# Reordered products, copies on either of two engines, and more buffers at the end of a fused attention and feed-forward kernel

## The chip, the core and the metric

The kernel runs on one core of a Trainium2 chip. A core has TensorE (PE in the profile, with its weight loads as PEld), VectorE (DVE), ScalarE (ACT), GpSimd (POOL) and SyncE (SP, which here only issues transfers). PE writes its sums to PSUM, of which this kernel uses eight banks; ACT and DVE read them from there. The engines run side by side, each through its own queue in a fixed order, and wait for one another by semaphores. The metric is the time of one execution in microseconds (us) as the device measures it; smaller is better. The span in a profile is some 1.8 us shorter than that time.

## The reference

```python
# q, k, v: 8 x 12 x 448 x 64; x: 3584 tokens x 768; d_ff = 2048
attn = softmax(rmsnorm(q) @ rmsnorm(k).T / 8) @ v
x = attn.transpose(0, 2, 1, 3).reshape(B * S, H * D)
h = x @ w_in
g = h * (1 / (1 + exp(-1.702 * h)))
return g @ w_out
```

The change touches only the last line and what surrounds it.

## The kernel before

For each batch of 448 tokens the kernel projects x (16 blocks of 6 matmuls), gets the gate as h * (1 + tanh(0.851 h)) with ACT and DVE, and multiplies by w_out with matmuls of 384 columns. The factor 0.5 comes with the copy out of PSUM. Attention for later batches runs between these matmuls.

`g @ w_out` is done for two tiles of 128 tokens at a time, as 2x2 blocks with seven products in place of eight. Four of the seven (P1, P6, P7, P4) add into one bank, and each intermediate value of that bank is itself needed. So it has to be copied out (X1, X2, X3) before the next product may add to it:

```python
def copy(name, tm, hf, after, **kw):                 # always on ACT
    od.add(name, "ACT", 490, lambda: copy_out(a, bp, tm, hf), ..., deps=[(*after, 1)], **kw)
def p6():
    multiply(P(6), a, S2, T2, False, None, [S2, X(1)] + terms)
    copy(X(2), t1, 1, P(6), takes=("osb", [...]))
def p7():
    multiply(P(7), a, S3, T3, False, None, [S3, X(2)])
    copy(X(3), t2, 1, P(7), takes=("osb", [...]))
    ...
def p4():
    multiply(P(4), a, A(3), T4, False, None, [X(3)])
    ...
def s():                                             # sums of gates, on DVE; 3 buffers
    summing(S1, A(2), A(3), ALU.add, b, (*P(5), 1))
    summing(S2, S1, A(0), ALU.subtract, b, (*P(6), 1))
    summing(S3, A(2), A(0), ALU.subtract, b, (*P(7), 1))
    summing(S4, A(1), S2, ALU.subtract, b, (*P(3), 1))
```

The products' order is written by hand for each kind of batch. A and B are the pairs, C is the one tile that has no partner, in four products; `s` stands for the sums:

```python
EVEN = ["s", 1, 2, 5, 6, 7, 4, 3]
FIRST = order("As A1 A2 A5 A6 Bs B1 A7 A4 A3 B2 B5 B6 B7 B4 B3")
MIDDLE = order("As A1 A2 A5 A6 C0 A7 C1 A4 A3 C2 Bs B1 B2 B5 B6 C3 B7 B4 B3")
FINAL = order("As A1 C0 A2 A5 A6 C1 A7 C2 Bs A4 A3 C3 B1 B2 B6 B5 B7 B8 B4")
```

Every operation goes as a task, with an estimated duration, to a planner in the kernel's own Python code. It plays the engines through, gives each free engine the ready task with the smallest key, and emits the instructions in the order in which it started them. The queues on the chip then run in that order, whatever the real times are. The planner keeps tasks marked `lock` (the sums are) away from POOL's work in its own timeline; nothing on the chip does.

## Time and profile before

| | before |
|---|---|
| time, median of the first 3 runs (range) | 433.37 us (432.29 to 433.52) |
| span of the profiled run | 431.6 us |
| PE busy | 412.6 us (96%), 3874 matmuls |
| DVE, ACT, POOL busy | 275.6, 317.2, 189.5 us |
| clock granted to PE (1.00 is full speed), first 17 us / from there to the last matmul | 0.90 / 1.00 |

The prediction below shows the lines that carry the argument. Beside them, the rows of the two instruction groups that empty PSUM. A row gives line, engine, operation, written<-read, shapes, count, then busy us, mean ns of one, and the engine's idle time before them with what ended most of it.

```profile
L961 ACT ACTIVATE osb<-w 128x384 f32<-128x384 f32 x45 | 22.1, 490 | 24.4 <-PE w L951 21.7
...
L965 DVE SCALAR_TENSOR_TENSOR osb<-w,osb 128x384 f32<-128x384 f32 x27 | 15.0, 554 | 20.4 <-PE w L951 11.0
```

Both engines mostly wait for PE here, as they should when PE sets the time.

### The profile page before, as it was taken

How to read it: one execution, taken by the hardware profiler on the slowest of the kernel's cores; microseconds unless marked ns; L12 is line 12 of the kernel's file. 1: busy time of each engine (PE TensorE's matmuls, PEld its weight loads, DVE VectorE, ACT ScalarE, POOL GpSimd, SP SyncE). 2: the span in 40 equal slices, each digit the busy share in tenths (PEclk: the TensorE clock that was granted, in tenths of full speed). 3: DMA queues.
4: the chain of work that ended last, by engine and by line, in shares of the span. 5: the costliest groups of instructions: out<-in, count | busy, mean ns of one | idle time of the engine just before them, and what ended most of it. 6: DMA issues, size and time to landing. Idle time of an engine off the chain costs nothing.

```text
span 431.6 us, 10059 instructions
## 1 busy us (share of the span) xinstructions
PE 412.6 (96%) x3874; PEld 242.7 (56%) x3874; DVE 275.6 (64%) x549; ACT 317.2 (73%) x472; POOL 189.5 (44%) x277
## 2 busy tenths in 40 slices
PE   6999899999999999999999899999999999999995
PEld 4558686655555555555555455555555555554553
DVE  4967988589977568857685447756564345635522
ACT  4798798869988889888877778878866676524221
POOL 5486943657648585463447353554624001000000
PEclk9899999999999999999999999999999999999999
DMA  9999999574795996785468895464326431030032
GB/s 208 240 257 245 257 247 248 139 163 99 162 211 149 208 229 144 182 190 153 97 158 192 167 202 120 118 173 119 83 73 152 99 90 21 12 85 0 18 93 73
DMA packets 101555, 63.38 MB, mean 147 GB/s; under 512 B 54916, under 2 KB 101508, under 8 KB 101508
## 3 DMA queue, kind: packets, MB, share of 16 engines
q1 hardware_dynamic: 93712, 55.88, 54.6%
q0 software_dynamic: 7296, 6.29, 8.9%
q8 instruction: 30, 0.49, 0.5%
q10 hardware_dynamic: 500, 0.57, 0.4%
q14 instruction: 17, 0.14, 0.1%
HBM read 45.61 MB, written 11.01 MB: 131 GB/s over the span
## 4 chain that ended last, share of the span: by engine, by line
PE 81%; ACT 6%; DVE 5%; DMA 4%; issue 2%; POOL 0%; SPq 0%; DVEq 0%; ACTq 0%; POOLq 0%
PE w L864 30%; PE w L951 20%; PE o L653 11%; PE sc L632 9%; PE w L894 4%; PE sc L951 3%; PE sc L864 3%; DMA raw<-in_k_dram 2%; ACT att L642 2%; ACT sq L514 1%; PE w L588 1%; ACT osb L961 1%; DVE g L886 1%; ACT att L640 1%; DVE late L942 1%
## 5 line engine op out<-in xcount | busy, mean ns | idle before, releaser
L640 ACT ACTIVATE att<-sc 112x896 bf16<-112x896 f32 x168 | 146.8, 924 | 23.5 <-PE sc L632 23.2
L864 PE MATMUL w<-xt,w_in_s 128*128 128x448 bf16 (+1 forms) x804 | 149.1, 330 | 0.5 <-DVE g L886 0.4
L864 PEld LDWEIGHTS <-w_in_s 128*128 128x128 bf16 x864 | 78.0, 97 | 53.3 <-issue 6.2
L565 POOL TENSOR_TENSOR row<-raw,rs 112x512 bf16<-112x512 f32 x80 | 86.5, 1103 | 29.6 <-DMA qk<-row 17.6
L653 PEld LDWEIGHTS <-att 112*128 112x128 bf16 x1536 | 72.0, 98 | 44.8 <-issue 19.0
L886 DVE SCALAR_TENSOR_TENSOR g<-th,w 128x448 bf16<-128x448 f32 x118 | 71.9, 616 | 28.9 <-ACT th L874 28.6
L874 ACT ACTIVATE th<-w 128x448 f32<-128x448 f32 x118 | 65.7, 558 | 23.6 <-PE w L864 20.5
L578 POOL TENSOR_TENSOR vx<-vraw,ones 112x512 bf16<-112x512 f32 x35 | 38.7, 1104 | 89.3 <-PE o L653 59.4
L653 PE MATMUL o<-vx,att 112*128 112x65 bf16 x1280 | 73.4, 194 | 1.1 <-DVE obs L664 1.0
L523 DVE TENSOR_REDUCE ssq<-sq 112x16 f32<-112x1024 f32 (+1 forms) x50 | 58.6, 1173 | 14.8 <-ACT sq L514 14.1
L514 ACT ACTIVATE sq<-raw 112x1024 f32<-112x1024 f32 (+1 forms) x43 | 44.8, 1041 | 10.1 <-DMA raw<-in_k_dram 6.2
L951 PEld LDWEIGHTS <-late 128*128 128x128 bf16 x376 | 33.7, 97 | 26.0 <-issue 7.6
L632 PE MATMUL sc<-qk 64*128 64x448 bf16 (+1 forms) x360 | 47.5, 344 | 0.9 <-DVE qk L595 0.5
L663 DVE RECIPROCAL rcp<-o 112x4 f32<-112x4 f32 x96 | 17.1, 178 | 43.6 <-PE o L653 43.4
L664 DVE TENSOR_TENSOR obs<-o,rcp 112x256 bf16<-112x256 f32 x96 | 40.7, 424 | 3.3
L951 PEld LDWEIGHTS <-g 128*128 128x128 bf16 x336 | 30.1, 97 | 22.2 <-issue 5.5
L961 ACT ACTIVATE osb<-w 128x384 f32<-128x384 f32 x45 | 22.1, 490 | 24.4 <-PE w L951 21.7
L951 PE MATMUL w<-w_out_s,g 128*128 128x384 bf16 x192 | 36.1, 326 | 0.0
L951 PE MATMUL w<-w_out_s,late 128*128 128x384 bf16 x168 | 32.8, 326 | 1.2 <-DVE osb L965 1.2
L951 PE MATMUL w<-late 128*128 128x384 bf16 x160 | 31.1, 326 | 1.2 <-ACT osb L961 1.2
L965 DVE SCALAR_TENSOR_TENSOR osb<-w,osb 128x384 f32<-128x384 f32 x27 | 15.0, 554 | 20.4 <-PE w L951 11.0
L555 POOL TENSOR_TENSOR t<-rs 112x48 f32<-112x48 f32 x28 | 8.2, 292 | 40.5 <-DVE rs L544 39.4
(77 smaller groups left out, 367.0 us busy)
## 6 DMA issues: line engine op xcount, KB each, us to landing
raw<-in_q_dram SPq DMA_DIRECT2D x44, 224.0 KB, 4.2
raw<-in_k_dram SPq DMA_DIRECT2D x43, 224.0 KB, 4.6
vraw<-in_v_dram SPq DMA_DIRECT2D x42, 224.0 KB, 3.8
w_in_s<-in_moe_w_in_dram POOLq DMA_DIRECT2D x4, 768.0 KB, 15.8
w_out_s<-in_moe_w_out_dram POOLq DMA_DIRECT2D x4, 768.0 KB, 21.6
out_dram<-osb SPq DMA_DIRECT2D x14, 168.0 KB, 2.5
out_dram<-osb SPq DMA_DIRECT2D x16, 144.0 KB, 2.3
out_dram<-osb SPq DMA_DIRECT2D x16, 120.0 KB, 2.7
```

The costliest lines, as they stand in the source:

```text
L514: nc.scalar.activation(out=sq[i % N_SQ][:SS, part], in_=raw[turn(i, N_RAW, K_RAW)][:SS, part], func=ACT.Square)
L523: nc.vector.reduce_sum(out=ssq_of[g0][:SS, i - g0, part], in_=sq[i % N_SQ][:SS, part], axis=AX.X)
L565: eng.tensor_tensor(out=row_ring[i % N_QKN][:SS, gi].rearrange("p n (h d) -> p h n d", h=2), in0=raw[turn(i, N_RAW, K_RAW)][:SS, gi], in1= ...
L578: nc.gpsimd.tensor_tensor(out=vx[:, :, :D], in0=vr, in1=ones[:SS, :].to_broadcast([SS, 2 * NS, D]), op=ALU.mult)
L632: nc.tensor.matmul(sc[:, hp, j * SH:j * SH + n], lhsT=qkw[r, k0:k0 + WIN], rhs=qk[r, 0, qs], start=True, stop=True)
L640: nc.scalar.activation(out=att[:SS, t, :, :S], in_=sc, func=ACT.Exp)
L653: nc.tensor.matmul(os_[u, w][:, x, :], lhsT=att_of(u)[:SS, kc, hp, qs * SS:qs * SS + WIN], rhs=vx_ring[turn(i, N_V, K_V)][:SS, hp, kc, :], ...
L664: nc.vector.tensor_tensor(out=to[:SS, :, w, :] if h is None else to[:SS, :2].rearrange("p n h d -> p (n h) d"), in0=o[:SS, :, :D], in1=rcp ...
L864: nc.tensor.matmul(gps[b, m][:, j * SH:j * SH + n], lhsT=w_in_s[:, ki, f * 128:(f + 1) * 128], rhs=xT[b][:, ki, lo:lo + n], start=(ki == 0 ...
L874: nc.scalar.activation(out=th[:, :], in_=gps[b, m][:, :S], func=ACT.Tanh, scale=0.851)
L886: nc.vector.scalar_tensor_tensor(out=g_of[b // 2][:, f:f + len(g), lo:lo + n], in0=view(ths.pop((b, m))[:, :]), scalar=1.0, in1=view(gps.p ...
L951: nc.tensor.matmul(held[to], lhsT=lhs[:, ko, :], rhs=y[:, ko, :], start=first and ko == 0, stop=ko == NK - 1, skip_group_check=not first)
```

## The change

The intent is that no product follows directly on the copy of its bank's partial sum. For that, half of C moves to the even batches, the next batch's first projection (D) is cut in two and pulled in, and the last batch interleaves A and B. A copy may run on ACT or DVE, whichever the planner finds free. Products wait for their own precomputed weight term only, and the subtractions that make those terms (`TT`) lose precedence. After attention, its idle buffers serve as more store buffers (osb) and sum buffers. The core of the diff:

```diff
-    EVEN = ["s", 1, 2, 5, 6, 7, 4, 3]
-    FIRST = order("As A1 A2 A5 A6 Bs B1 A7 A4 A3 B2 B5 B6 B7 B4 B3")
-    MIDDLE = order("As A1 A2 A5 A6 C0 A7 C1 A4 A3 C2 Bs B1 B2 B5 B6 C3 B7 B4 B3")
-    FINAL = order("As A1 C0 A2 A5 A6 C1 A7 C2 Bs A4 A3 C3 B1 B2 B6 B5 B7 B8 B4")
+    FIRST = order("As A1 A2 A5 A6 Bs B1 A7 A4 A3 B2 B5 B6 D0 B7 D1 B4 B3")
+    EVEN = order("As A1 A2 A5 A6 C0 A7 C1 A4 A3")
+    MIDDLE = order("As A1 A2 A5 A6 C2 A7 C3 A4 A3 Bs B1 B2 B5 B6 D0 B7 D1 B4 B3")
+    FINAL = order("As A1 B1 A2 A5 A6 C2 A7 Bs C3 A4 A3 B2 B6 B5 B7 B8 B4")
 ...
-                   deps=[(*after, 1)], **kw)
+                   deps=[(*after, 1)], either=("DVE", 560, lambda: copy_out_v(a, bp, tm, hf)), **kw)
 ...
-            multiply(P(7), a, S3, T3, False, None, [S3, X(2)])
+            multiply(P(7), a, S3, T3, False, None, [S3, X(2)] + term(0))
 ...                                                  # likewise P5, P6, P4
-                           10.3 + done / PACE - 2, lock=True,          # the terms TT
+                           10.3 + done / PACE + TERM_LATE, lock=True,  # TERM_LATE = 1.0
 ...
+            od.add("later", "none", 0, lambda: None, 0,
+                   widen=[("osb", len(osb_ring)), ("sums", len(sums))],
+                   deps=last_values(NG - 1))
```

(`...` marks cuts; the copies of `C` get the same choice of engine.) The rest of the diff teaches the planner to offer one task to two engines and to pick the buffer that has been free longest.

More of the change, by code (lines that the diff above doesn't have):

```diff
@@ L20 @@
 class _Task:
-    __slots__ = ("eng", "dur", "lat", "emit", "key", "after", "at", "takes", "left", "users", "end", "start", "lock", "widen", "moves", "rest", "there", "alt")
+    __slots__ = ("eng", "dur", "lat", "emit", "key", "after", "at", "takes", "left", "users", "end", "start", "lock", "widen", "moves", "rest", "there", "alt", "either")
 OVERLAP = {"ACT": 95.0, "DVE": 90.0, "POOL": 45.0}
@@ L41, in add @@
     def add(self, name, eng, dur, emit, key, deps=(), lat=100.0, at=0.0, takes=None,
-            lock=False, widen=None, moves=None, alt=None):
+            lock=False, widen=None, moves=None, alt=None, either=None):
         t = _Task()
@@ L57, in add @@
         t.moves = moves
+        t.either = either and (either[0], either[1] - OVERLAP[either[0]],
+                               lat - OVERLAP.get(eng, 0.0) + OVERLAP[either[0]], either[2])
         t.key = KEYS.get(name, round(key, 3))
@@ L127, in run @@
                         c = heapq.heappop(q)
+                        if c[2].end is not None:
+                            continue
                         if self._fits(c[2], now):
@@ L135, in run @@
                         break
+                    if best.either and eng != best.eng:
+                        best.eng, best.dur, best.lat, best.emit = best.either
+                    best.either = None
                     if best.takes and best.takes[0] in self.loose:
@@ L142, in run @@
                         self.slots[best.takes[0]][1].extend(best.takes[1])
-                    if best.widen:
-                        self.slots[best.widen[0]][0] = best.widen[1]
+                    for name, n in best.widen or ():
+                        self.slots[name][0] = n
                         self.fill = None
@@ L177, in run @@
                 for u in t.users:
-                    if (u.eng == t.eng) == same:
+                    if (u.eng == t.eng and not u.either) == same:
                         u.left -= 1
@@ L184, in run @@
                 seq += 1
-                heapq.heappush(ready[t.eng], (t.key, seq, t))
+                for eng in (t.eng, t.either[0]) if t.either else (t.eng,):
+                    heapq.heappush(ready[eng], (t.key, seq, t))
         move_to(now + 1e6)
@@ L460 @@
     th_p = pool("th", 3)
-    osb_p = pool("osb", 6)
+    osb_ring = ring("osb", 6, [128, HALF], FP32)
+    for t in att_ring:
+        flat = t[:, :, :, :].rearrange("p n h q -> p (n h q)").bitcast(FP32)
+        osb_ring += [flat[:, j * HALF:(j + 1) * HALF] for j in range(NS)]
     ps_sc = pool("ps_sc", 1, space=PSUM)
@@ L468 @@
         od.slot(name, n)
-    od.loose = ("w",)
+    od.loose = ("w", "osb", "sums")
     banks = [ps_w.tile([128, 512], FP32, tag=f"w{j}", name=f"w{j}") for j in range(3)]
@@ L923 @@
     sums = [piece(S_LEN).rearrange("p (k t) -> p k t", k=NK) for _ in range(N_SUM)]
+    for t in sq:
+        flat = t[:, :, :, :, :].rearrange("p g h n d -> p (g h n d)").bitcast(BF16)
+        sums += [flat[:, j * S_LEN:(j + 1) * S_LEN].rearrange("p (k t) -> p k t", k=NK)
+                 for j in range(2)]
     B11, T1, B21, B22 = [w_out_s[:, NK * r:NK * r + NK, hf * HALF:(hf + 1) * HALF]
@@ L932 @@
     od.slot("sums", N_SUM)
-    sum_of, summed = {}, [0]
+    sum_of = {}
     def tokens(bp, tm, r):
@@ L938, in add_up @@
     def add_up(name, x, y, op):
-        sum_of[name] = sums[summed[0] % N_SUM]
-        summed[0] += 1
+        sum_of[name] = sums[od.got]
         x, y = (sum_of[t] if t in sum_of else tokens(*t) for t in (x, y))
@@ L956, in half_of @@
         if (bp, tm, hf) not in osbs:
-            osbs[bp, tm, hf] = osb_p.tile([128, HALF], FP32, tag="osb", name="osb")
+            osbs[bp, tm, hf] = osb_ring[od.got]
         return osbs[bp, tm, hf][:, :]
@@ L961, in copy_out, with copy_out_v @@
         nc.scalar.mul(half_of(bp, tm, hf), held[frm], 0.5)
+    def copy_out_v(frm, bp, tm, hf):
+        nc.vector.tensor_scalar(out=half_of(bp, tm, hf), in0=held[frm], scalar1=0.5, scalar2=None,
+                                op0=ALU.mult)
     def add_out(frm, bp, tm, hf):
@@ L973 @@
     PACE = 5800.0
+    TERM_LATE = 1.0
     END = (B // 2 - 1, 2 * S // 128 - 1)
-    EVEN = ["s", 1, 2, 5, 6, 7, 4, 3]
     order = lambda text: [(p[0], int(p[1]) if p[1:].isdigit() else p[1]) for p in text.split()]
-    FIRST = order("As A1 A2 A5 A6 Bs B1 A7 A4 A3 B2 B5 B6 B7 B4 B3")
-    MIDDLE = order("As A1 A2 A5 A6 C0 A7 C1 A4 A3 C2 Bs B1 B2 B5 B6 C3 B7 B4 B3")
-    FINAL = order("As A1 C0 A2 A5 A6 C1 A7 C2 Bs A4 A3 C3 B1 B2 B6 B5 B7 B8 B4")
+    FIRST = order("As A1 A2 A5 A6 Bs B1 A7 A4 A3 B2 B5 B6 D0 B7 D1 B4 B3")
+    EVEN = order("As A1 A2 A5 A6 C0 A7 C1 A4 A3")
+    MIDDLE = order("As A1 A2 A5 A6 C2 A7 C3 A4 A3 Bs B1 B2 B5 B6 D0 B7 D1 B4 B3")
+    FINAL = order("As A1 B1 A2 A5 A6 C2 A7 Bs C3 A4 A3 B2 B6 B5 B7 B8 B4")
     done = 0.0
@@ L982 @@
     last_sum = None
+    rest = []
     def plain(bp, b, tm, hf):
@@ L1032, in pair @@
         A = lambda j: (bp, (t1, t2)[j // 2], j % 2)
-        terms = [("TT", j, r) for j in range(4) for r in range(2)]
+        term = lambda j: [("TT", j, r) for r in range(2)]
         U = lambda tm, hf: ("U", bp, tm, hf)
@@ L1054, in p5 @@
         def p5():
-            multiply(P(5), c, S1, T1, True, U(t1, 1), [S1] + terms)
+            multiply(P(5), c, S1, T1, True, U(t1, 1), [S1] + term(1))
         def p6():
-            multiply(P(6), a, S2, T2, False, None, [S2, X(1)] + terms)
+            multiply(P(6), a, S2, T2, False, None, [S2, X(1)] + term(2))
             copy(X(2), t1, 1, P(6), takes=("osb", [("D", bp, t1, 1)]))
         def p7():
-            multiply(P(7), a, S3, T3, False, None, [S3, X(2)])
+            multiply(P(7), a, S3, T3, False, None, [S3, X(2)] + term(0))
             copy(X(3), t2, 1, P(7), takes=("osb", [("D", bp, t2, 1)]))
@@ L1067, in p4 @@
         def p4():
-            multiply(P(4), a, A(3), T4, False, None, [X(3)])
+            multiply(P(4), a, A(3), T4, False, None, [X(3)] + term(3))
             copy(U(t2, 0), t2, 0, P(4), takes=("osb", [("D", bp, t2, 0)]))
@@ L1106, in part @@
                        10.3 + done / PACE - 2, deps=[(*y[j], 1)],
+                       either=("DVE", 560, lambda: copy_out_v(to[hf], bp, tm, hf)),
                        takes=("osb", [("D", bp, tm, hf)]))
@@ L1110, in single, with project @@
         return [lambda j=j: part(j) for j in range(4)]
+    def project(b, m, kis):
+        nonlocal done, last
+        name = ("F", b, m) if kis[-1] == KI - 1 else ("F", b, m, kis[0])
+        od.add(name, "PE", len(kis) * 191, lambda: first(b, m, kis), 10.3 + done / PACE,
+               deps=[("X", b * NP + p, None if b else m // 8) for p in kis]
+               + [("WI", blocks(b, m)[0][0] // 4), last],
+               lat=250, takes=("w", [("G", b, m)]) if kis[0] == 0 else None,
+               widen=[("w", 3)] if b == m == 0 else None)
+        last = name
+        done += len(kis) * 191
     for b in range(B):
@@ L1115 @@
             key = 10.3 + done / PACE
-            od.add(("F", b, m), "PE", KI * 191, lambda b=b, m=m: first(b, m, range(KI)), key,
-                   deps=[("X", b * NP + p, None if b else m // 8) for p in range(KI)]
-                   + [("WI", blocks(b, m)[0][0] // 4), last],
-                   lat=250, takes=("w", [("G", b, m)]),
-                   widen=("w", 3) if b == m == 0 else None)
-            last = ("F", b, m)
-            done += KI * 191
+            if ("F", b, m) not in od.named:
+                project(b, m, range(KI))
             od.add(("H", b, m), "ACT", 542, lambda b=b, m=m: tanh(b, m), key - 2,
@@ L1131 @@
         if b == B - 1:
-            od.add("late", "none", 0, lambda: None, 0, widen=("w", len(banks)),
+            od.add("late", "none", 0, lambda: None, 0, widen=[("w", len(banks))],
                    deps=[("E", NG - 1, None, t) for t in range(NS)])
+            od.add("later", "none", 0, lambda: None, 0,
+                   widen=[("osb", len(osb_ring)), ("sums", len(sums))],
+                   deps=last_values(NG - 1))
         if b == 0:
@@ L1148 @@
                 one, two = pair(bp, b, 3, 4), pair(bp, b, 5, 6)
-                rest = single(bp, b, 2) if bp else []
+                next_first = [lambda kis=range(j, j + KI // 2): project(b + 1, 0, kis)
+                              for j in (0, KI // 2)]
                 for part in (FINAL if b == B - 1 else MIDDLE) if bp else FIRST:
-                    {"A": one, "B": two, "C": rest}[part[0]][part[1]]()
+                    {"A": one, "B": two, "C": rest, "D": next_first}[part[0]][part[1]]()
                 before_g = [last, last_sum]
@@ L1154 @@
                 one = pair(bp, b, 0, 1)
-                for j in EVEN:
-                    one[j]()
+                rest = single(bp, b, 2) if b > 0 else []
+                for part in EVEN:
+                    {"A": one, "C": rest}[part[0]][part[1]]()
     global _last_order
```

## The prediction

> **What bounds the kernel now.** I read the busy shares, the chain that ended last, what TensorE (PE) waits for after 94 us, and then the order of time around each wait. The first two say that PE sets the time:
>
> ```profile
> PE 412.6 (96%) x3874; PEld 242.7 (56%) x3874; DVE 275.6 (64%) x549; ACT 317.2 (73%) x472; POOL 189.5 (44%) x277
> ...
> PE 81%; ACT 6%; DVE 5%; DMA 4%; issue 2%; POOL 0%; SPq 0%; DVEq 0%; ACTq 0%; POOLq 0%
> ```
>
> The span is 431.6 us, so PE is idle for 19.0 us. By stretches of the span, 7.0 us of that lie before 70 us (the filling of the pipeline), 4.3 us after 425 us (the last copy and stores), and about 7.7 us in between, where the products that the change orders run (line L951, from 122 us on). PE's clock is full from 20 us on. No matmul goes away, so the change can win only what PE loses in between. Who holds PE up from 94 us on (total us, times, longest):
>
> ```profile
> PE w L951 <- ACT osb L961: 3.3, 5, 1.5
> PE w L951 <- DVE osb L965: 1.2, 2, 0.6
> PE o L653 <- DVE obs L664: 1.0, 1, 1.0
> PE sc L951 <- DVE osb L965: 0.7, 1, 0.7
> PE sc L951 <- ACT osb L961: 0.6, 1, 0.6
> PE w L864 <- DVE g L886: 0.4, 1, 0.4
> ```
>
> Nine waits, 5.8 us, are for a copy (L961) or an addition (L965) out of PSUM. This undercounts: a matmul of 384 columns is drawn 0.326 us long, but the next starts 0.162 us after it. From start to start, beyond that pitch, the nine cost 0.74 (at 144 us), 0.75 (236), 1.68 (245), 0.48 (283), 0.74 (336), 0.48 (379), 0.74 (381), 0.74 (419) and 0.87 us (421): 7.24 us in all. This is the ceiling for the reordering. One of them in order of time, products A6, A7 and A4 of batch 6, all on one bank:
>
> ```profile
> 378.73 1.46 PE L951 MATMUL w<-late 128*128 128x384 bf16 x8 [0.32 <-ACT osb L961]
> ...
> 380.22 0.49 ACT L961 ACTIVATE osb<-w 128x384 f32<-128x384 f32 x1 [1.55 <-PE w L951]
> ...
> 380.76 1.46 PE L951 MATMUL w<-late,g 128*128 128x384 bf16 x8 [0.58 <-ACT osb L961]
> ```
>
> A7 ends its last pitch near 380.02, the copy starts 0.2 us later, takes 0.49, and A4, which adds into the same bank, starts 0.05 us after that: 0.74 us lost each time a product follows its own partial sum's copy. The longest wait has another cause:
>
> ```profile
> 243.85 1.06 ACT L514 ACTIVATE sq<-raw 112x1024 f32<-112x1024 f32 x1 [1.34 <-DMA raw<-in_k_dram]
> ...
> 244.81 0.47 ACT L961 ACTIVATE osb<-w 128x384 f32<-128x384 f32 x1
> ...
> 245.34 1.46 PE L951 MATMUL w<-late,g 128*128 128x384 bf16 x8 [1.52 <-ACT osb L961]
> ```
>
> Here the copy sat in ACT's queue behind a square that waited for a load. At 236 and 336 us PE waits for an addition that frees one of the three banks: the single tile's sum (C2, C3) holds a bank across B1, B2 and B5. At the end two waits follow each other in the chain:
>
> ```profile
> 418.60 0.50 ACT osb L961
> 419.10 1.60 issue
> 420.69 0.57 DVE osb L965
> 421.26 0.04 issue
> 421.30 3.42 PE sc L951 x20
> ```
>
> B1 ended at 417.75, but its copy started at 418.60, 0.2 us after the fourth matmul of B2, and B2's fifth waited for that copy. B1 and B2 lay in the two halves of one two-bank sc tile, and the waits look set for the whole tile.
>
> **What the Trainium skill says.** "Perfetto Trace Analysis", section Matmuls, says that independent groups should rotate through different PSUM banks, so that one's evacuation overlaps the next one's matmuls. The trace agrees: only products that need the bank or the sum being read stop (0.74 us). "ScalarE: Activation LUTs", section What ACT_TABLE_LOAD costs, gives an ACTIVATE with immediate scale and bias 186 ns + 0.833 ns per element: 506 ns for 384, where the trace has 490. For a copy on DVE there is no row of before; the addition L965 reads the same bank and takes 554 ns, so I take 0.56 us. "PSUM — Partial Sum Buffer", section on bank collisions, wants guards by bank, not by address; the waits at 419 us are coarser still, by tile of two banks.
>
> **The change part by part.** It adds and removes no matmul (projecting a batch's first block in two halves of 3 matmuls keeps all 6), so PE's work stays as it is.
>
> 1. Even batches 2, 4 and 6 run "A6 C0 A7 C1 A4" for "A6 A7 A4". A product of 8 x 0.162 = 1.30 us covers the 0.2 + 0.49 + 0.05 = 0.74 us of a copy. The waits at 283, 379 and 381 us go: -1.7 us.
> 2. The odd batches before the last get the single tile's rest between A's products, so no third bank is held across B. The waits at 236 and 336 us go: -1.5 us.
> 3. "B6 D0 B7 D1 B4" puts 3 projection matmuls, 3 x 0.189 = 0.57 us, after a copy that needs 0.74 to 0.81. At 144 us some 0.2 us stay, -0.5. At 245 us the cause was a queue; the cover and the free choice of engine should take half to all of 1.68: -0.9. The projection's input lands in time: the last transposes before these points landed near 139 and 237 us, D1 comes near 146 and 244.
> 4. The last batch: B1 comes early, so its copy is long done when B2 and B6 run, -0.74. B6 still follows B2 at once, and the addition out of B2's bank can stop it again if both lie in one sc tile; I count half of 0.87, -0.4.
> 5. The terms' subtractions on DVE (8 of 1.0 to 1.2 us) lose their precedence over the gates of batch 1. PE waited for gates at 104 (0.29 us) and 110 us (0.73 us), beside these subtractions. -0.7. Each product now waits only for its own term, which permits this.
> 6. Copies on DVE: up to all 50, 50 x 0.56 = 28 us on an engine busy for 276 of 432. It fits. In the last copy of all it could cost 0.07 us.
> 7. More store and sum buffers, only once attention is over. ACT waited 6.4 us for stores near the end, but PE then had other banks: 0. The sums let S4 of B come sooner; PE never waited for it: 0.
>
> A cost: in batches 3 and 5 the order is now "A5 A6 C2", with still three sum buffers. C2's sum S5 comes after S4 in DVE's order; S4 gets the buffer that A5 frees, so S5 gets the one that A6 frees. C2 follows A6 directly, so it starts 0.2 + 0.69 (one L942 addition) + 0.05 = 0.94 us late, unless attention's matmuls fill the hole. Two such places, half filled: +1.0 us. For new accidents in the queues, like the one at 245 us, I add 0.5 us.
>
> Sum: 1.7 + 1.5 + 1.4 + 1.1 + 0.7 = 6.4 saved, 1.5 lost; net 4.9, from 433.4 to 428.5 us. Half of the accidents and refills may go well, so I put the middle at 428.2.
>
> **The rivals.** (a) Everything goes: the nine waits, the two for gates and the one for obs (1.16 us from start to start, at 281 us) are 9.4 us: 424.0 us. For it: PE's queue is otherwise full, attention offers work until 380 us. Against it: the order is fixed ahead from estimated times, and a static order always meets a late load somewhere. (b) The wait moves: C2 waits for S5, DVE's copies queue behind reductions that wait for ACT's squares (1.22 us each), projections hold banks longer, sc tiles collide more often. Then 3 to 4 us come back: 430 to 432 us. For it: DVE is 78% busy from 94 to 150 us, and the S5 dependence is plain in the code. (c) Attention becomes the bound, since products move forward from odd to even batches and projections are pulled up. ACT is 92% busy from 94 to 150 us. If projections then wait for transposes, 434 us or more. Against it: the input lands about 7 us before the pulled-up projections, and even batches get 2.6 us more time before the next projection.
>
> **Range and chances.** PE's removable loss bounds the win at 9.4 us, 2.2%; going 2% faster, below 424.7 us, needs nearly all of it, hence 0.04. Slower by 2%, above 442, needs a new stall bigger than any in this trace: 0.02. Repeats of before lie within 1.2 us, so the range comes from how many waits return: 425.5 to 431.5 us, the lower end with about 8 us won, the upper with about 2.
>
> **What would show it.** PE's waits for L961 and L965 should fall from 5.8 us to under 2, with none in even batches and none near 236 or 336 us. PE's busy time should stay within 1 us of 412.6, with the same 3874 matmuls. The new DVE copies should take 0.54 to 0.57 us, and L961's count fall by their number. A wait of C2 on L942 in batches 3 and 5, near 220 and 320 us, would show the cost I added. The tail after the last matmul should stay about 4.4 us. I am wrong if PE waits for transposes or gates more than before, if sc-tile waits in the last 30 us grow, or if the early part before 94 us shifts: the change should leave it as it is.

## The result

The changed kernel took 428.34 us (median of 4 runs, 428.1 to 428.48), the kernel before, on the same chip, 432.91 us. The ratio is 0.9894, with a 95% interval of 0.9876 to 0.9912. Such a ratio is the mean time of one kernel's runs over that of the other's of the same rounds, so it is not quite the ratio of the medians. It is faster by about 1%, clear of noise, and the forecast was 428.2 us.

The added code shifts the line numbers. In the kernel before, L951 is a product of `g @ w_out`, L961 a copy, L965 an addition out of PSUM, L942 a sum of gates, L653 attention's product with v, and L664 the division that follows it. In the changed kernel these are L965, L975 (copy on ACT) and L978 (copy on DVE), L983, L956, L664 and L675. L864 and L875 are the projection.

From the page of the changed kernel (span, busy times, shares of the chain that ended last):

```profile
span 426.3 us, 10048 instructions
...
PE 409.1 (96%) x3874; PEld 241.7 (57%) x3874; DVE 297.3 (70%) x584; ACT 302.6 (71%) x437; POOL 189.8 (45%) x277
...
PE 78%; DVE 11%; ACT 5%; issue 3%; DMA 2%; POOL 0%; DVEq 0%
```

PE still sets the time, with the same 3874 matmuls. The 35 copies that moved show as 35 more instructions on DVE (549 to 584) and 35 fewer on ACT (472 to 437). DVE's share of the chain rose from 5 to 11%. What PE waited for from 94 us on points to the reason (us in total, times, longest; it is the whole answer).

```profile
PE o L664 <- DVE obs L675: 4.7, 7, 1.2
PE w L965 <- DVE late L956: 0.2, 1, 0.2
```

All nine waits for copies and additions are gone. Seven waits for attention's division (obs) have come in place of one. In the chain after 94 us, sums of gates rose from 3.6 to 15.8 us. The end, where the chain before had copies, additions and "issue" between the products, is now one unbroken row of products. The chain of the changed kernel from 400 us on (start, us, what):

```profile
401.18 1.30 PE w L965 x8
402.48 2.60 PE sc L965 x16
...
418.08 3.91 PE sc L965 x24
421.99 0.02 issue
422.02 0.56 DVE att L978
```

**A measure that leaves out the start.** The first 1082 matmuls are the same in both kernels, yet the two profiled runs were already 1.27 us apart at the hundredth. The windows show the granted clock in the first 17 us as 0.90 in the run of before and 1.00 in the other. So 1.27 of the 5.2 us between the two spans is chance. From the thousandth matmul's start to the last one's, I get 339.98 us before and 335.91 after: the change itself is worth 4.07 us. This measure repeats well: the changed kernel gave 335.91 and 335.94 in two profiles on two occasions, and the kernel of e7 and e11 gave 331.19 both times. It holds where PE's clock stays full.

**Where those 4.07 us come from.** Each figure is the time from one matmul's start to the next beyond the usual pitch of that pair, summed by what ended the wait:

| PE lost, us (times) | before | after |
|---|---|---|
| copies and additions (L961, L965 / L975, L978, L983) | 7.23 (9) | 0 |
| attention's division (obs) | 1.16 (1) | 5.87 (7) |
| sums (L942 / L956) | 0 | 0.32 (1) |
| gates | 1.36 (4) | 0.24 (1) |
| other waits | 0.76 (4) | 0 |
| sum | 10.51 | 6.43 |

The difference is 4.08 us, which is all of it as far as this method can tell: waits of 0.1 us lie at its edge, so the row of others could be a few tenths larger or smaller. The change did what it was made for, and over half of the gain went into a new wait.

**The new wait, one place.** Timeline of the changed kernel in batch 2 (start, us, engine, line, operation, shapes, count, idle before and releaser):

```profile
176.25 3.94 POOL L576 TENSOR_TENSOR row<-raw,rs 112x512 bf16<-112x512 f32 x3
...
176.81 1.02 DVE L956 TENSOR_TENSOR late<-g 128x1024 bf16<-128x1024 bf16 x1
...
177.87 1.42 DVE L956 TENSOR_TENSOR late<-late,g 128x1024 bf16<-128x1024 bf16 x1
...
179.21 1.53 DVE L956 TENSOR_TENSOR late<-g 128x1024 bf16<-128x1024 bf16 x1
...
180.66 0.54 DVE L983 SCALAR_TENSOR_TENSOR osb<-w,osb 128x384 f32<-128x384 f32 x1
...
181.33 0.42 DVE L675 TENSOR_TENSOR obs<-o,rcp 112x256 bf16<-112x256 f32 x1
...
181.81 0.43 PE L664 MATMUL o<-vx,att 112*128 112x65 bf16 x8 [0.82 <-DVE obs L675]
```

The same three sums in the kernel before:

```profile
177.06 0.69 DVE L942 TENSOR_TENSOR late<-g 128x1024 bf16<-128x1024 bf16 x1
177.78 0.69 DVE L942 TENSOR_TENSOR late<-late,g 128x1024 bf16<-128x1024 bf16 x1
178.39 0.68 DVE L942 TENSOR_TENSOR late<-g 128x1024 bf16<-128x1024 bf16 x1
```

The planner takes 690 ns for a sum. That holds while POOL is idle, as it was before until 178.65 us. Beside POOL's work the three took 1.02, 1.42 and 1.53 us. They stand ahead of the division in DVE's queue, with an addition of 0.54 us between, and attention has one PSUM bank, which the division frees. Six of the seven waits, 5.5 of 5.87 us, have two or three sums ahead of the division, at least one of them slow; in four of the six an addition stands there too. Before the seventh (0.34 us, at 323 us) DVE was idle. "SBUF — State Buffer", section Who interferes with whom, says that a DVE instruction with two SBUF inputs contends with a GpSimd instruction that reads SBUF, and that the loser is blocked outright. The traces agree that they contend (whether the loser is blocked or only slowed, durations alone do not tell): of the 53 sums in both profiles that no POOL instruction overlaps, none took more than 0.694 us. Of the 41 that one overlaps, 29 took 0.74 to 1.55 us. Eleven sums before and 16 after took over 0.8 us. POOL's instructions are slowed too: L576 takes 1.04 us by the median and up to 1.5 us beside sums in the changed kernel. No run took POOL's work away, so that POOL is the cause rests on this overlap and on the page.

### The profile page after: what moved, and what is told of

The parts are those of the page before. It is cut to its first block, busy times and chain, and to the rows that moved or that the text cites. A ratio compares the mean times of both kernels' runs of the same rounds, so it can differ in the third digit from the quotient of the medians.

```text
span 426.3 us, 10048 instructions
## 1 busy us (share of the span) xinstructions
PE 409.1 (96%) x3874; PEld 241.7 (57%) x3874; DVE 297.3 (70%) x584; ACT 302.6 (71%) x437; POOL 189.8 (45%) x277
## 4 chain that ended last, share of the span: by engine, by line
PE 78%; DVE 11%; ACT 5%; issue 3%; DMA 2%; POOL 0%; DVEq 0%
PE w L875 30%; PE w L965 17%; PE o L664 10%; PE sc L643 9%; PE sc L965 4%; PE w L905 4%; DVE late L956 4%; PE sc L875 2%; ACT att L653 2%; ACT sq L525 1%; DVE ssq L534 1%; DVE obs L675 1%; DVE g L897 1%; DMA raw<-in_k_dram 1%; DVE w_out_s L945 1%
## 5 line engine op out<-in xcount | busy, mean ns | idle before, releaser
L875 PE MATMUL w<-xt,w_in_s 128*128 128x448 bf16 (+1 forms) x810 | 150.7, 330 | 0.1
L875 PEld LDWEIGHTS <-w_in_s 128*128 128x128 bf16 x864 | 78.1, 97 | 54.2 <-issue 6.7
L576 POOL TENSOR_TENSOR row<-raw,rs 112x512 bf16<-112x512 f32 x80 | 89.5, 1139 | 25.8 <-DMA qk<-row 13.5
L664 PEld LDWEIGHTS <-att 112*128 112x128 bf16 x1536 | 72.5, 98 | 49.3 <-issue 18.2
L885 ACT ACTIVATE th<-w 128x448 f32<-128x448 f32 x119 | 64.6, 548 | 26.3 <-PE w L875 24.7
L664 PE MATMUL o<-vx,att 112*128 112x65 bf16 x1280 | 74.2, 194 | 4.9 <-DVE obs L675 4.7
L589 POOL TENSOR_TENSOR vx<-vraw,ones 112x512 bf16<-112x512 f32 x35 | 36.5, 1042 | 95.0 <-PE o L664 59.4
L675 DVE TENSOR_TENSOR obs<-o,rcp 112x256 bf16<-112x256 f32 x96 | 40.8, 425 | 3.3
L965 PEld LDWEIGHTS <-g 128*128 128x128 bf16 x336 | 29.9, 97 | 19.6 <-issue 3.0
L965 PEld LDWEIGHTS <-late 128*128 128x128 bf16 x328 | 28.8, 97 | 18.3 <-issue 2.6
L965 PE MATMUL w<-w_out_s,g 128*128 128x384 bf16 x176 | 33.5, 325 | 0.0
L965 PE MATMUL w<-w_out_s,late 128*128 128x384 bf16 x152 | 29.7, 326 | 0.2 <-DVE late L956 0.2
L965 PE MATMUL w<-late 128*128 128x384 bf16 x144 | 28.1, 326 | 0.0
L978 DVE TENSOR_SCALAR osb<-w 128x384 f32<-128x384 f32 x25 | 13.9, 557 | 16.8 <-PE w L965 16.8
L617 ACT ACTIVATE qk<-qk,gG 128x448 bf16<-128x448 bf16 x36 | 24.2, 676 | 0.3 <-DMA qk<-row 0.3
## 6 DMA issues: line engine op xcount, KB each, us to landing
w_in_s<-in_moe_w_in_dram POOLq DMA_DIRECT2D x4, 768.0 KB, 15.8
```

What stands on the lines that cost most here:

```text
L576: eng.tensor_tensor(out=row_ring[i % N_QKN][:SS, gi].rearrange("p n (h d) -> p h n d", h=2), in0=raw[turn(i, N_RAW, K_RAW)][:SS, gi], in1= ...
L589: nc.gpsimd.tensor_tensor(out=vx[:, :, :D], in0=vr, in1=ones[:SS, :].to_broadcast([SS, 2 * NS, D]), op=ALU.mult)
L664: nc.tensor.matmul(os_[u, w][:, x, :], lhsT=att_of(u)[:SS, kc, hp, qs * SS:qs * SS + WIN], rhs=vx_ring[turn(i, N_V, K_V)][:SS, hp, kc, :], ...
L675: nc.vector.tensor_tensor(out=to[:SS, :, w, :] if h is None else to[:SS, :2].rearrange("p n h d -> p (n h) d"), in0=o[:SS, :, :D], in1=rcp ...
L875: nc.tensor.matmul(gps[b, m][:, j * SH:j * SH + n], lhsT=w_in_s[:, ki, f * 128:(f + 1) * 128], rhs=xT[b][:, ki, lo:lo + n], start=(ki == 0 ...
L885: nc.scalar.activation(out=th[:, :], in_=gps[b, m][:, :S], func=ACT.Tanh, scale=0.851)
```

## The experiments

Theory A: the reordering removed the waits for copies, and the new waits come from slow sums ahead of the division in DVE's queue. Theory B: the copies moved to DVE keep the division waiting. A further rival for the gain: the free choice of engine, not the order, removed the waits. The table sums up all twelve runs; "1000 to last" is the measure above, "copies", "obs" and "sums" what PE lost, all in us from the one profiled run. Waits for gates and other waits are left out of it, and entries of 0.2 us and less say little.

| run | median us (n) | ratio to before [95%] | 1000 to last | copies | obs | sums |
|---|---|---|---|---|---|---|
| changed kernel | 428.34 (4) | 0.9894 [0.9876, 0.9912] | 335.91 | 0 | 5.87 | 0.32 |
| e1 copies on ACT only | 426.98 (4) | 0.9856 [0.9820, 0.9892] | 334.19 | 0 | 4.53 | 0 |
| e2 old order | 433.12 (4) | 0.9992 [0.9953, 1.0031] | 340.77 | 5.91 | 2.13 | 0 |
| e3 terms first | 427.56 (4) | 0.9862 [0.9829, 0.9895] | 334.82 | 0 | 2.80 | 0.32 |
| e4 no more buffers | 429.80 (4) | 0.9919 [0.9887, 0.9951] | 337.37 | 0 | 5.49 | 1.27 |
| e5 changed kernel again | 428.91 (6) | 0.9897 [0.9872, 0.9923] | 335.94 | 0 | 5.99 | 0.32 |
| e6 ACT only, terms first | 427.29 (5) | 0.9863 [0.9835, 0.9891] | 333.93 | 0.15 | 2.71 | 0.32 |
| e7 planner's sum at 1300 | 424.12 (4) | 0.9795 [0.9761, 0.9829] | 331.19 | 0 | 0.68 | 1.19 |
| e8 S3 early | 427.72 (5) | 0.9869 [0.9841, 0.9897] | 335.95 | 0.88 | 2.49 | 1.19 |
| e9 before, sum at 1300 | 430.87 (6) | 0.9939 [0.9913, 0.9965] | 338.59 | 5.04 | 0 | 0 |
| e10 e6 with sum at 1300 | 424.88 (5) | 0.9802 [0.9779, 0.9826] | 331.60 | 0 | 0.90 | 0.19 |
| e11 e7 again | 423.59 (5) | 0.9780 [0.9757, 0.9804] | 331.19 | 0 | 0.68 | 1.19 |
| e12 no pull-up | 427.99 (6) | 0.9874 [0.9850, 0.9898] | 333.92 | 0 | 3.86 | 0.32 |

e1 to e4, e5 to e8 and e9 to e12 each shared a chip and the runs of the kernel before (medians 433.30, 433.41 and 432.89 us). All gave correct results.

### e1: copies on ACT only

```diff
-                   deps=[(*after, 1)], either=("DVE", 560, lambda: copy_out_v(a, bp, tm, hf)), **kw)
+                   deps=[(*after, 1)], **kw)
```

(The same for the single tile's copies.)

> The changed kernel with every copy back on ACT (no choice of engine), all else kept. Its trace shows that PE's waits for copies are gone and that PE now waits 5.9 us from start to start (4.7 us as idle time) for the division of attention (obs). Theory A: those waits come from the sums, which run 1.0 to 1.5 us in place of 0.69 where they meet POOL's work and stand ahead of the division in DVE's queue; the copies on DVE have little to do with it. Then the waits for obs stay at 4 to 6 us, the order alone covers the copies, and the time stays within 1.2 us of 428.3. Theory B: the 35 copies moved to DVE (19.5 us) are what keeps the division waiting; then obs waits fall under 2 us and the time to about 424.5 us.

No wait for a copy came back: the order covers copies on ACT just as well. The obs waits stayed at 4.53 us, as theory A expects, and B's 424.5 us was not reached. The time, 426.98 us, fell 1.3 us below 428.3, just outside A's 1.2 us. Obs waits are 1.3 us less than in the changed kernel, which is most of the 1.7 us by which this kernel's trace is shorter; sums slower than 0.8 us fell from 16 to 11. So the free choice of engine is no gain here.

### e2: the old order

```diff
-    EVEN = order("As A1 A2 A5 A6 C0 A7 C1 A4 A3")
+    EVEN = order("As A1 A2 A5 A6 A7 A4 A3")
```

(And FIRST, MIDDLE and FINAL as before, C in odd batches only.)

> The changed kernel with the order of the products as before (single tile in odd batches, projection not pulled up), but with copies on either engine, terms later, and more buffers at the end. If the order is what removed the nine waits for copies and additions (7.24 us), they come back save those that a queue or the few buffers caused (1.7 us at 245 us, perhaps 0.7 at the end): PE waits 4 to 6 us for them, and the time is 431.5 to 434 us. If the free choice of engine did it, PE waits under 2 us for them and the time is near 428.5 us.

PE's waits for L978 and L983, the copies and additions on DVE, in this kernel (att is attention's buffer, used here for a copy) from 94 us on:

```profile
PE w L965 <- DVE att L978: 1.4, 2, 0.8
PE w L965 <- DVE osb L983: 1.1, 2, 0.6
PE w L965 <- DVE osb L978: 0.8, 2, 0.4
PE sc L965 <- DVE att L978: 0.7, 1, 0.7
PE sc L965 <- DVE att L983: 0.6, 1, 0.6
```

Seven of the nine are back at their old places (238, 282, 335, 377, 380, 419 and 421 us, 4.96 us from start to start), now behind copies and additions on DVE, and one of 0.95 us is new at 410 us: 5.91 us. The two at 144 and 245 us, 2.42 us before, did not come back, so it did not take the new order to remove these two. The time, 433.12 us, is that of the kernel before, which a new wait of 1.78 us for a gate at 199 us helped to bring about. So the rest of the change without the order won nothing here, and for seven of the nine waits the order is what removed them.

### e3: the terms at their old precedence

```diff
-    TERM_LATE = 1.0
+    TERM_LATE = -2.0
```

> The changed kernel with only the terms' subtractions back at their old precedence on DVE. The gate waits near 104 and 110 us (1.0 us together) should come back, so the time is 0.5 to 1.2 us above 428.3. If they were an accident of that one trace, the time stays within 0.4 us of the changed kernel's.

The gate waits came back where they had been, 0.29 us at 103 and 0.46 us at 109 us, and a third, of 0.76 us, came at 260 us. But the obs waits fell from 5.87 to 2.80 us, and the trace is 1.1 us shorter, not longer. The miss is mine: the part does what I said, but the later waits changed by more than it is worth.

### e4: no added buffers

```diff
-            od.add("later", "none", 0, lambda: None, 0,
-                   widen=[("osb", len(osb_ring)), ("sums", len(sums))],
-                   deps=last_values(NG - 1))
```

> The changed kernel without the added store and sum buffers at the end. My prediction gave them 0 us in the old order. In the new order the single tile's third product follows A6 directly, and with three sum buffers its sum S5 waits for A6: I expect a PE wait of about 0.9 us near 405 us and a time 0.5 to 1.5 us above 428.3. If the store buffers matter as well, copies wait for stores and PE for them: over 2 us above.

One line of this kernel's waits answers it:

```profile
PE sc L965 <- DVE late L956: 0.8, 1, 0.8
```

At 409.04 us C2 started 0.95 us late, waiting for its sum S5, which had to wait for the buffer that A6 frees. No wait for store buffers reached PE. The trace is 1.46 us longer than the changed kernel's, of which this wait is 0.95. The intervals of the two ratios overlap, so the trace decides here.

### e5: the changed kernel again

> The changed kernel itself, as a control on the chip on which the next three run: 428.3 us within 0.7, PE's waits for obs 4.5 to 5 us of idle time, 15 or 16 of 47 sums slower than 0.8 us.

As expected: a ratio of 0.9897, the same waits to within 0.12 us, 16 slow sums.

### e6: copies on ACT only and terms first

The edits of e1 and e3 together.

> Copies on ACT only and the terms at their old precedence, both together: the order and the buffers alone. The two alone measured 427.0 and 427.6 beside 428.3 us for the whole change (on another chip). If both parts of the change cost time (each by putting work ahead of the division in DVE's queue), together they give 426.0 to 427.2 us and obs waits under 3 us. If those differences were chance, the time is that of the control within 0.5 us.

At 427.29 us it missed the range of 426.0 to 427.2 us by 0.1 us; the obs waits, 2.71 us, are as expected. By the trace, 2.0 us shorter than the control's, the order and the buffers alone do at least as well as the whole change; the intervals of the two ratios overlap.

### e7: the planner's figure for a sum

```diff
-        od.add(name, "DVE", 690, lambda: add_up(name, x, y, op), 10.3 + done / PACE - 2, lock=True,
+        od.add(name, "DVE", 1300, lambda: add_up(name, x, y, op), 10.3 + done / PACE - 2, lock=True,
```

> The changed kernel, with the planner told that a sum takes 1300 ns in place of 690, which is what it measures where POOL runs beside it. No instruction is added; the planner then sees the division become ready before the third sum and puts it first. Theory A (slow sums ahead of the division): obs waits fall under 2.5 us and the time by 1.5 to 3.5 us, to 425 to 427 us. If the order in DVE's queue is not the cause, the waits stay at 4 us or more.

It beat the forecast: 424.12 us. From its timeline at batch 1:

```profile
121.37 1.07 DVE L956 TENSOR_TENSOR late<-g 128x1024 bf16<-128x1024 bf16 x1
...
122.47 1.42 DVE L956 TENSOR_TENSOR late<-late,g 128x1024 bf16<-128x1024 bf16 x1
...
124.02 0.42 DVE L675 TENSOR_TENSOR obs<-o,rcp 112x256 bf16<-112x256 f32 x1
...
124.82 0.68 DVE L956 TENSOR_TENSOR late<-g 128x1024 bf16<-128x1024 bf16 x1
```

The first two sums are as slow as in the changed kernel (1.07 and 1.42 us there too). But the division now stands before the third, and PE's wait of 1.41 us at this place is gone. Over the whole kernel the obs waits fell from 5.99 (e5) to 0.68 us; the trace shortened by 4.75 us. A new wait of 1.0 us for a sum near 224 us is the price.

The queue's order is only one half of this. Of the six places where sums had held up the division, it comes before the third sum at three (batch 1, and near 217 and 315 us). At the other three it still follows the same sums, but these took only 0.68 to 0.81 us (near 217 and 315 us they were faster as well). At batch 2, where they had taken 1.02, 1.42 and 1.53 us:

```profile
174.42 0.81 DVE L956 TENSOR_TENSOR late<-g 128x1024 bf16<-128x1024 bf16 x1
175.27 0.69 DVE L956 TENSOR_TENSOR late<-late,g 128x1024 bf16<-128x1024 bf16 x1
175.88 0.68 DVE L956 TENSOR_TENSOR late<-g 128x1024 bf16<-128x1024 bf16 x1
```

The planner lets no POOL task start while a `lock` task runs in its timeline, so the larger figure also keeps POOL away for longer: slow sums fell from 16 to 9. Batch 1 is direct evidence for the order in the queue, batch 2 for the slow sums; how the 4.75 us divide between the two was not measured.

### e8: the third sum early

```diff
+            summing(S3, A(2), A(0), ALU.subtract, b, (*P(7), 1), upto=NK)
             summing(S1, A(2), A(3), ALU.add, b, (*P(5), 1))
             summing(S2, S1, A(0), ALU.subtract, b, (*P(6), 1))
-            summing(S3, A(2), A(0), ALU.subtract, b, (*P(7), 1))
```

(`upto` limits the gates that the sum waits for.)

> The changed kernel with the sum S3 first and waiting only for the half of the gates that it reads (it needs none of the upper half), so that it runs during the projection and not between it and the products. It takes one of the three sums (0.7 to 1.5 us) out of DVE's queue at the place where the division waits: the five longest obs waits (1.4, 1.0, 1.0, 0.5, 1.1 us) should each shrink by that much, leaving 1 to 2 us in all, and the time should fall by 3 to 4 us, to 424.5 to 425.5 us (theory A). If DVE's copies and additions are what stands there (theory B), the waits fall by less than half and the time by less than 1.5 us.

This fell short. The obs waits fell to 2.49 us, but sums took 1.19 and an addition 0.88 us (at 375 us: the shared two-bank tile again). The profile is also disturbed. In windows around 230 us (us, PE busy, PEld, DVE, ACT, POOL, granted clock, DMA share, GB/s):

```profile
224.00:228.50 4.50, 2.89 (x43) 1.72 (x44) 2.26 (x6) 3.72 (x5) 3.92 (x10) 0.99 0.89 145
228.50:232.00 3.50, 3.50 (x13) 1.63 (x11) 0.95 (x1) 1.33 (x2) 2.38 (x3) 0.52 0.91 200
232.00:236.00 4.00, 4.00 (x30) 2.48 (x28) 3.43 (x5) 2.02 (x3) 2.04 (x2) 1.00 0.73 219
```

PE ran at half its clock for 3.5 us, which cost some 1.7 us from start to start, so the trace would be near 334.3 us without it. The gain is then 1.2 us by the medians and 1.7 us by the trace. The obs waits fell by more than half, which is against B, but the time by far less than A's 3 to 4 us. So the run does not separate A from B.

### e9: the kernel before with the planner's sum at 1300

The edit of e7 in the kernel before.

> The kernel before, with only the planner's figure for a sum set to 1300 ns in place of 690. In its trace one wait for the division cost 1.16 us from start to start and the copies cost 7.24. If slow sums ahead of the division are what the new order ran into (theory A), this can win about 1 us at most here: 432 to 433.5 us beside 433.4. If the figure helps whatever the order (by moving DVE's work about), it wins 3 us or more, as it did in the changed kernel (428.9 to 424.1).

It won 1.4 us in the trace, 2.0 us by the medians and 2.6 us by the ratio, more than A's "1 us at most" and less than the rival's 3. The obs wait (1.16 us) went, and so did the accident at 245 us (1.68) and the wait at 283 us, while new waits for gates and for ACT came. So the figure won something in the old order too, and 4.75 us in the new one.

### e10: e6 with the planner's sum at 1300

> Order and buffers of the change, copies on ACT only, terms at their old precedence, and the planner's sum at 1300 ns. With the sum at 690 this measured 427.3 beside 428.9 us for the whole change. If the two gains add, 423.0 us; if both remove the same waits for the division, about 424.1 us, as with the figure alone.

424.88 us, nearer to 424.1 than to 423.0: the gains do not add, and the obs waits are down to 0.90 us as in e7 (0.68). With the figure at 1300, copies on either engine and late terms (e7) are 0.4 us better in the trace than copies on ACT and early terms, the reverse of e6 against e5.

### e11: e7 again

> The changed kernel with the planner's sum at 1300 ns again, as a control and to narrow the interval: 424.1 us within 0.7, ratio to before 0.978 to 0.981.

423.59 us, ratio 0.978. Its waits from 94 us on:

```profile
PE w L965 <- DVE late L956: 0.8, 1, 0.8
PE o L664 <- DVE obs L675: 0.4, 2, 0.2
```

This kernel beats both: 9.3 us under the kernel before by the medians of this call, and in e7's call 4.8 us under the changed kernel.

### e12: no pulled-up projection

```diff
-    FIRST = order("As A1 A2 A5 A6 Bs B1 A7 A4 A3 B2 B5 B6 D0 B7 D1 B4 B3")
+    FIRST = order("As A1 A2 A5 A6 Bs B1 A7 A4 A3 B2 B5 B6 B7 B4 B3")
```

(MIDDLE likewise.)

> The changed kernel without the pulled-up projection (batches 1, 3 and 5 end in B6 B7 B4 B3 as before), all else kept. My step 3 puts the pull-up at 1.4 us: 0.5 us at 144 us and 0.9 us at 245 us. If so, PE waits again for copies of B6 or B7 in batches 1, 3 or 5, 0.7 to 2.2 us in all, and the time is 0.7 to 2.2 us above the changed kernel, a ratio to before of 0.991 to 0.995. If attention's matmuls cover those copies anyway, the ratio stays at 0.989 to 0.990.

No wait for a copy over 0.1 us came back, and the ratio, 0.9874, is below both expectations. At 143 us, between B6 and B7, the planner put 16 value matmuls and 4 score matmuls of attention where D0 had been, and they cover the copy of 0.56 us. The trace is 2.0 us shorter than the changed kernel's, which equals its lower obs waits (3.86 for 5.87 us). The pull-up is not needed.

## Why the prediction was right or wrong

The time (428.2 against 428.34 us) and the range were right. The sum behind them was not as right as its total: gains and losses were both larger than I put them, so that the total came within 0.2 us is partly luck.

- **The bound.** Right: PE's queue sets the time, and only its waits could be won. The nine waits were the right list (7.23 us; the prediction wrote 7.24). Its sentence that only products which need the bank or the sum being read stop does not hold for two of them, at 419 and 421 us, where a copy or an addition of one bank stopped a product into the other half of its tile. One sign named beforehand did not come: PE's busy time was to stay within 1 us of 412.6 and fell to 409.1 us, 2.2 us of it before the thousandth matmul, where the run of before had the lower clock, and 1.3 us after.
- **Step 1, even batches, -1.7.** Right. The three waits are gone; in the old order (e2) they return with 1.92 us (at 282, 377 and 380 us).
- **Step 2, no bank held across B, -1.5.** Right: the waits at 236 and 336 us are gone and return in e2 with 1.43 us.
- **Step 3, the pulled-up projection, -1.4.** The two waits went, but the pull-up was not needed for it. e12 lacks it and has neither, and so does e2, which has the old order altogether. In e12 attention's matmuls cover the copy, which I had not looked for; at 144 us before, products had followed each other with none between.
- **Step 4, the last batch, -1.1.** Both waits (0.74 and 0.87 us) went, so 1.6. The shared two-bank tile did not stop B6; in e2 and e8 such waits are there again (0.81 to 0.88 us each), e8 having the new order. So the order alone does not rule them out; probably it depends on which banks the planner picks, which was not tested.
- **Step 5, the terms, -0.7.** The term was mis-sized and its net effect missed. The gate wait at 110 us cost 0.45 us beyond the usual pitch; 0.73 was the whole step from start to start. So the two are worth 0.73 before together, and one of 0.24 us is left. Rival (a)'s 9.4 us are 9.1 for the same reason. In e3 the whole kernel is 1.1 us better in the trace without this part, as its later obs waits are lower.
- **Step 6, copies on DVE.** The duration was right (0.557 us against 0.56), the count was 35 and not up to 50. "It fits" was right for the sum of work. That e1's trace is 1.7 us shorter without them suggests that room on an engine is not the whole question. Between e10 and e11, which also differ in the terms, the sign is the opposite, so no fixed price can be put on them.
- **Step 7, more buffers, 0.** Wrong. I judged the sums by the old order. In the new one C2 follows A6 directly in the last batch too, and three buffers cost a wait of 0.95 us there (e4). I had named just this dependence for batches 3 and 5 and had not applied it to the last.
- **C2 behind S5 in batches 3 and 5, +1.0.** Mis-sized: 0.32 us in batch 3 and no such wait in batch 5. The planner filled the hole with attention.
- **New accidents, +0.5.** This is the step that failed: it was put at 0.5 us, and the obs waits alone grew by 4.7 us. Rival (b) had named DVE's queue as the place, but with reductions and copies as the cause; the traces and e7 show sums that run up to 2.2 times their planned time beside POOL and stand ahead of the division. The profile of before had the sign: one obs wait at 281 us, right behind sums of 1.55 and 1.42 us.

I counted 6.4 us saved and 1.5 us lost, net 4.9. In the trace 7.2 us of copies, 1.1 us of gates and 0.8 us of others went, and 5.0 us of obs and sums came, net 4.1. The two errors nearly cancelled.

**What stays open.** Why the new order meets POOL's work more often is not settled. Slow sums number 11 before, 16 in the changed kernel, 15 in e4, and 10 to 13 in e1, e3, e6, e8 and e12, each a small edit of it; their number alone does not set the obs waits (10 slow sums in e8 with 2.49 us, 10 in e12 with 3.86). Part of it may be that this one plan falls badly; the new order's obs waits are 2.5 to 6.0 us in all versions with the sum at 690 ns, against 1.16 us before and 2.13 us in e2. So a difference of 1 to 2 us between two of these versions can't be put down to the edited part's own work.

## What to carry to other kernels

When a queue's order is planned ahead, feed the plan the durations measured under the contention that the operation really meets: here one figure (690 to 1300 ns) won 4.75 us in the trace, where the whole change had won 4.07. After removing a wait, read the next one's releaser and see what stands before it in that engine's queue, as busy time won't show it. And compare traces from a common instruction on, so that chance at the start is not taken for an effect.

## What the Trainium skill lacked or had wrong

- "SBUF — State Buffer", section Who interferes with whom, has the contention that decided this case, and the runs agree that the two contend. It gives no size for such a pair (its 6.8 and 1.5 times belong to measurements whose instructions it does not name). Here a 128x1024 bf16 sum took 0.68 to 0.69 us alone and up to 1.55 us beside POOL, whose 112x512 instructions took 1.04 us by the median and up to 1.5 us beside sums in the changed kernel.
- "PSUM — Partial Sum Buffer" asks for guards by bank. No page says that waits may be set for a whole two-bank tile: a copy of one bank waited for a product into the other and held up its second half, 0.74 and 0.87 us before, 0.88 us in e8.
- "ScalarE: Activation LUTs", section What ACT_TABLE_LOAD costs, has a formula from which I estimate 506 ns for the copy (the prediction's 506 ns is the same estimate); the runs show 490.
- "TensorE: Matmul & The Clock Gate", section What's actually happening, ties the half clock to idle windows of about 3.4 us and does not say how idle a window must be. In e8 the granted clock was half from 228.4 to 231.9 us. In the 3.4 us before, PE's longest wait was 0.85 us, and its two longest came to 1.6 us together. What caused the fall was not tested.
